# Attention in quarters of the TensorE array, interleaved score by value, in a fused attention and feed-forward kernel

## The chip, the cores and the metric

One core of a Trainium2 chip runs the whole program. The metric is the device time of one execution in microseconds; where several executions are given, it is their median.

## What is computed

```
q_n, k_n = rmsnorm(q, g_q), rmsnorm(k, g_k)       # 8 batches x 12 heads x 448 rows x 64, f32
scores   = q_n @ k_n.T / 8
attn     = exp(scores - max) / sum(exp(scores - max))
x        = (attn @ v), heads side by side          # 3584 x 768
h        = max(x @ w_in, 0)                        # 3584 x 2048
out      = (h * h) @ w_out                         # 3584 x 768
```

Everything is f32.

## The kernel before

**Units.** Attention is cut into 48 units `i` of two heads `e` (one batch, heads 2c and 2c+1). Scores are made transposed: keys on the partitions, the 448 queries along the row. The 448 keys of a head are three slots `m` of 128 keys and a rest of 64 keys; the rests of an even unit and of the odd one behind it share a fourth slot `NJ` (number 3). `score` (L426) multiplies kT by qT for both heads of a slot into two PSUM banks chosen by `banks_of` (L421), `weigh` (L439) has ScalarE (ACT) write exp of them to two `wT` tiles, `attend` (L506) multiplies v by these weights one unit later and adds over the slots in bank 4 (`values_bank`, L503). No maximum is subtracted in the branch that runs (`shift=False`); the gains are small enough. The sums of the weights are added up by GpSimd (POOL, `add_up`, L454), spread by matmuls with ones (`both_denominators`, L570, for two units at once), turned and moved out of PSUM by VectorE (DVE, `take_sums`, L604), inverted (`invert_both`, L579) and multiplied into x (`finish`, L647).

**Tiles of the array.** With 64 rows of d to contract, the two heads of a score use the upper and the lower 64 rows of the array at the same time, each with 128 columns (shape 64\*128). The values contract 128 keys and give 64 columns a head, so the two heads use the left and the right half (128\*64). The denominators use four strips of 32 columns (128\*32). Slot `NJ` uses quarters (64\*64), in `score` and in `attend_both` (L527). An f32 matmul stands in the trace as two records.

**The other work.** The feed-forward part uses products in the manner of Strassen: `first_products` or `deep_products` (L953; L982 is their matmul), then `second_products` (L1106; matmuls L1160, and L1098 in `multiply_rest`). These run in four blocks for each pair of batches, as a generator `ffn(u)`; DVE adds most products to SBUF (L1217, L967), ACT copies some (L979, L971). `deep_products` uses a bank aside, `banks[free_bank]`; `multiply_rest` uses banks 2 and 1. Banks 5 to 7 take the products in turn (`roles`).

**Order.** One program order is written out by hand. The main loop (L1690) runs the feed-forward generator up to a point (`run`, L1462, by planned costs and `place`, L1448), then makes one visit. Units up to 24 are visited in halves; from unit 25 on (`whole`, L275), one visit (`visit_whole`, L1640) does the scores of unit i and the values of unit i-1. Visits 25 to 47 are of this kind, visit 48 has the values of unit 47 alone. Three visits fall into each block; one of the three comes just behind `multiply_rest`. Visits 25 and 37 fall on the end of a pair of batches, where the generator is drained first.

Small work (turning q and k of the next unit, L365 on DVE and L367 on ACT; squares and their sums for a unit further on, L179 on ACT and L192 on DVE; inverting) stands in a deque `tasks`. One or two of these are issued with each step of the generator. `run_all` (L1487), at the start of each visit, issues all that are left. Between two points of each block the tasks are held back (`held`, L1057 to L1154), and the visit behind `multiply_rest` is the first to run them.

In `visit_whole` before, the order for TensorE is: scores of slots 0 and 1; values of slots 0, 1, 2 of the unit before; for odd i the values of slot `NJ` for units i-1 and i (`attend_both`), for even i the denominators of units i-2 and i-1; then the score of slot 2, and for even i of slot `NJ`. Scores use banks 0 to 3. For odd i, ACT then copies bank 0 and bank 4 to SBUF (L1661, L1663); the values of the odd unit are joined with that rest by DVE in `finish` (L652), as a task behind the next visit.

**Transfers.** All of them are issued by SyncE (SP), on one hardware queue. `transfers_of` (L310) puts a transfer in a list that is followed some at a time, one or two with each step of the generator. Loads of v (`load_v`, L370) go through that list; each is two transfers and one or two of `lasts`. `load_out` (L856) brings 1.5 MB of output weights and is issued directly, two calls for the next block, two steps after the end of a block (L1209, the list `later`).

## Time and profile before

| | us |
|---|---|
| median of 3 runs (1427.46 to 1429.78) | 1429.35 |
| profiled execution | 1425.93 |
| its span | 1424.1 |
| TensorE clock granted, share of full | 0.995 |
| TensorE matmul (PE) busy | 1389.0 |
| GpSimd (POOL) busy | 782.6 |
| VectorE (DVE) busy | 824.7 |
| ScalarE (ACT) busy | 583.2 |

The profile's page gives busy times, then the chain of work that ended last, then groups of instructions by line and shape. Ends of matmuls are modelled and overlap, so the starts of neighbouring matmuls are the better clock. A shape "64\*128 64x448" is a matmul with 64 rows and 128 columns of the array and 448 columns streamed.

### The profile page before, as it was taken

Reading aid. Unit: us, or ns where it says so; the run is one execution under the profiler, and the core shown is the slowest. Engines: PE = TensorE matmul, PEld = TensorE weight load, DVE = VectorE, ACT = ScalarE, POOL = GpSimd, SP = SyncE. Lnnn points to the kernel's source line nnn. Section 1 sums busy time; section 2 is a strip of 40 time slices with the busy share of each in tenths; the row PEclk is TensorE's granted clock in tenths of the full one; section 3 lists DMA queues with packets and bytes.
Section 4 is the critical chain, followed back from the end, with each engine's and each line's share of the span. In section 5 each row is a group of like instructions: output and inputs, shape, how many; then the busy total and the mean of one; then the engine's idle time right before and its main releaser. Section 6 shows DMA issues by size and latency. Waiting matters only on the chain.

```text
span 1424.1 us, 18297 instructions
## 1 busy us (share of the span) xinstructions
PE 1389.0 (98%) x5772; PEld 837.1 (59%) x5772; DVE 824.7 (58%) x1651; ACT 583.2 (41%) x1126; POOL 782.6 (55%) x778
## 2 busy tenths in 40 slices
PE   7999999999999999999999999999999999999998
PEld 3333444444444467584756757576675858778694
DVE  5997466877888854354444664344543565254444
ACT  6775466645646234452333423444333403221220
POOL 5666755654655877566574876655663654030311
PEclk9999999999999999999999999999999999999999
DMA  5555836857859875482736548374541716234132
GB/s 144 144 153 159 205 94 163 249 166 185 261 132 266 252 237 139 97 254 66 224 106 210 155 115 263 80 214 125 183 126 34 274 58 243 109 106 174 45 144 81
DMA packets 378927, 229.09 MB, mean 161 GB/s; under 512 B 271940, under 2 KB 347588, under 8 KB 374724
## 3 DMA queue, kind: packets, MB, share of 16 engines
q1 hardware_dynamic: 378528, 227.75, 55.1%
q8 instruction: 48, 0.79, 0.2%
q14 instruction: 59, 0.48, 0.1%
q10 hardware_dynamic: 292, 0.07, 0.0%
HBM read 172.49 MB, written 55.25 MB: 160 GB/s over the span
## 4 chain that ended last, share of the span: by engine, by line
PE 80%; DMA 4%; DVE 4%; POOL 3%; issue 3%; ACT 3%; SPq 3%; POOLq 0%; DVEq 0%; ACTq 0%
PE bank L1160 30%; PE bank L982 23%; PE bank L434 8%; PE bank L521 7%; PE bank L1098 5%; PE bank L928 4%; DMA vt<-in_v_dram 2%; DMA words<-in_moe_w_out_dram 1%; POOL sum L461 1%; SPq L316 1%; PE bank L533 1%; ACT wT L442 1%; PE bank L573 1%; PE bank L564 1%; DVE out_sb L1290 1%
## 5 line engine op out<-in xcount | busy, mean ns | idle before, releaser
L1217 DVE TENSOR_TENSOR acc<-acc,bank 128x384 f32<-128x384 f32 x324 | 173.9, 550 | 205.4 <-PE bank L1160 176.9
L982 PE MATMUL bank<-xT,in_sb 128*128 128x224 f32 x1344 | 288.0, 353 | 0.0
L1160 PE MATMUL bank<-out_sb,hid 128*128 128x384 f32 x768 | 270.9, 490 | 3.2 <-DVE acc L1217 2.5
L982 PEld LDWEIGHTS bank<-xT,in_sb 128*128 128x128 f32 x1344 | 252.7, 190 | 10.3 <-issue 3.9
L442 ACT ACTIVATE wT<-bank,rr 128x448 f32<-128x448 f32 x288 | 161.6, 631 | 124.6 <-PE bank L434 103.2
L1160 PE MATMUL bank<-out_sb,sums 128*128 128x384 f32 x576 | 207.4, 491 | 2.0 <-DVE acc L1217 1.9
L202 POOL TENSOR_TENSOR rr<-ms,minus_half 128x8 f32<-128x8 f32 (+1 forms) x96 | 147.8, 1540 | 111.7 <-DVE ms L195 90.1
L1160 PEld LDWEIGHTS bank<-out_sb,hid 128*128 128x128 f32 x768 | 145.0, 191 | 108.4 <-issue 6.5
L967 DVE TENSOR_TENSOR hid<-hid,bank 128x224 f32<-128x224 f32 x312 | 111.6, 383 | 128.8 <-PE bank L982 109.4
L434 PE MATMUL bank<-qT,kT 64*128 64x448 f32 (+1 forms) x768 | 172.5, 579 | 5.4 <-ACT part L442 3.4
L1160 PEld LDWEIGHTS bank<-out_sb,sums 128*128 128x128 f32 x576 | 107.5, 190 | 87.4 <-issue 6.9
L928 PE MATMUL bank<-xT,in_sb 128*128 128x448 f32 x336 | 131.9, 546 | 0.2 <-DVE hid L1068 0.2
L434 PEld LDWEIGHTS bank<-qT,kT 64*128 64x128 f32 (+1 forms) x768 | 59.3, 174 | 108.6 <-issue 70.2
L1035 POOL TENSOR_TENSOR hid<-hid 128x448 f32<-128x448 f32 x24 | 27.4, 1140 | 169.4 <-DVE hid L967 154.7
L461 POOL TENSOR_TENSOR sum<-sum,wT 128x448 f32<-128x448 f32 (+1 forms) x96 | 112.8, 1196 | 8.7 <-ACT wT L442 8.1
L521 PE MATMUL bank<-wT,vt 128*64 128x448 f32 x480 | 105.0, 550 | 3.7 <-DMA vt<-in_v_dram 3.7
L928 PEld LDWEIGHTS bank<-xT,in_sb 128*128 128x128 f32 x336 | 62.1, 190 | 69.2 <-issue 59.7
L461 POOL TENSOR_TENSOR sum<-wT 128x448 f32<-128x448 f32 x48 | 56.9, 1195 | 81.6 <-PE bank L573 80.7
L1039 ACT ACTIVATE hid<-hid 128x448 f32<-128x448 f32 x96 | 54.9, 572 | 83.5 <-DVE hid L967 54.2
L1098 PE MATMUL bank<-out_sb,hid 128*128 128x384 f32 x256 | 87.6, 488 | 0.0
L367 ACT ACTIVATE qT<-qT,g 128x448 f32<-128x448 f32 x34 | 22.7, 667 | 146.6 <-DVE qT L365 146.6
L982 PE MATMUL bank<-more,in_sb 128*128 128x224 f32 x288 | 74.4, 353 | 0.0
(130 smaller groups left out, 1854.4 us busy)
## 6 DMA issues: line engine op xcount, KB each, us to landing
out_sb<-out_forms SPq DMA_DIRECT2D x24, 1536.0 KB, 9.1
in_sb<-in_deep SPq DMA_DIRECT2D x64, 384.0 KB, 4.4
in_sb<-in_deep SPq DMA_DIRECT2D x80, 256.0 KB, 4.5
words<-in_moe_w_in_dram SPq DMA_DIRECT2D x32, 384.0 KB, 3.8
words<-in_moe_w_out_dram SPq DMA_DIRECT2D x32, 384.0 KB, 3.5
out_forms<-out_sb SPq DMA_DIRECT2D x8, 1536.0 KB, 6.6
qk<-in_q_dram SPq DMA_DIRECT2D x96, 96.0 KB, 2.8
qk<-in_k_dram SPq DMA_DIRECT2D x96, 96.0 KB, 2.8
```

What stands on the lines that cost most here:

```text
L202: self.nc.gpsimd.tensor_tensor(out=self.rr[i][:, x, 0 : self.count(i)], in0=ms, in1=self.minus_half.to_broadcast(list(ms.shape)), op=ALU.pow,)
L434: nc.tensor.matmul(sc[some], lhsT=turned[p, 1][r, keys], rhs=turned[p, 0][r, :], start=True, stop=True,)
L442: nc.scalar.activation(new_weights((i, m), e), sc, AF.Exp, scale=rows.rr[i][:, 1, 2 * m + e : 2 * m + e + 1],)
L461: nc.gpsimd.tensor_tensor(out=sums[i, e][some], in0=left[some], in1=weights[key_of(i, m), e][some], op=ALU.add)
L521: nc.tensor.matmul(values_bank(i)[ds(e * D, D), :], lhsT=lasts[i % 2][mine, e, :] if m == NJ else values[i][:, m, e, :], rhs=weights[key_o ...
L928: nc.tensor.matmul(ps, lhsT=w_sb[:, IN.index(left), c, :], rhs=forms[u, c][right], start=first and c == 0, stop=c == NK - 1, skip_group_ch ...
L967: nc.vector.tensor_tensor(out=quarter(name, n), in0=quarter(base, n), in1=ps, op=ALU.add)
L982: nc.tensor.matmul(ps, lhsT=left, rhs=right, start=start, stop=stop, skip_group_check=True)
L1039: nc.scalar.activation(dst, dst, AF.Relu)
L1098: nc.tensor.matmul(ps, lhsT=hid[a].rearrange("p t e s -> p t (e s)")[:, t, ds(NT * P, P)], rhs=w_sb[t][:, 2 * a + half, :], start=(a, t) = ...
L1160: nc.tensor.matmul(ps, lhsT=lefts[left][:, t, ts(tt, P)], rhs=w_sb[t][:, OUT.index(right), :], start=first and t == 0, stop=t == 1, skip_g ...
L1217: nc.vector.tensor_tensor(out=acc, in0=acc, in1=ps, op=ALU.add)
```

## The change

In visits from 25 on (and not in the other branch, `shift`):

- `score` makes slots 0 to 2 with four matmuls of 64\*64, by head and by half of the 128 keys.
- `attend_halves` makes the values of slots 0 to 2 with four matmuls of 64\*64, by half of the keys and by head; the lower 64 keys add up in bank 4, the upper 64 in bank 3. `join_halves` adds both banks (and the rest) in the visit itself.
- Values and scores alternate slot by slot. The denominators of an even visit come first, and in bank 2. Scores use banks (0, 1), (2, 0), (1, 2) and, for `NJ`, (0, 4).
- `free_bank` stays 1.
- `load_v` issues its transfers directly once the first pair of batches is through; `load_out` comes four steps behind a block, not two.

```
 def load_v(i):
-        queue = transfers_of("v", i)
+        queue = transfers_of("v", i) if first else nc.sync
...
 def banks_of(i, m):
-        first = 2 * m - 3 if whole(i) and m > 1 else m % 2 * 2
-        return [banks[(first + e) % 4][:, 0:S] for e in range(2)]
+        if whole(i) and not shift:
+            return [banks[n][:, 0:S] for n in ((0, 1), (2, 0), (1, 2), (0, 4))[m]]
+        return [banks[m % 2 * 2 + e][:, 0:S] for e in range(2)]
...
 def score(i, m):
+        if whole(i) and m < NJ:
+            for e, sc in enumerate(scs):
+                for half in range(2):
+                    nc.tensor.matmul(
+                        sc[ds(half * D, D)],
+                        lhsT=turned[i, 1][ds(e * D, D), ds(m * P + half * D, D)],
+                        rhs=turned[i, 0][ds(e * D, D), :], start=True, stop=True,
+                    )
+            return
...
+    def attend_halves(i, n):
+        for half, bank in enumerate((values_bank(i), second_bank(i))):
+            keys = ds(half * D, D)
+            for e in range(2):
+                nc.tensor.matmul(
+                    bank[ds(e * D, D), :], lhsT=values[i][keys, n, e, :],
+                    rhs=weights[(i, n), e][keys], start=n == 0, stop=n == NJ - 1 and (half or i % 2) == 1,
+                )
+    def join_halves(i):
+        xT = xts[pairs[i]] = new_x()
+        if i % 2:
+            nc.vector.tensor_tensor(out=xT, in0=values_bank(i), in1=rests.pop(i), op=ALU.add)
+        else:
+            nc.scalar.copy(rests[i + 1], banks[0][:, 0:S])
+            nc.scalar.copy(xT, values_bank(i))
+        nc.vector.tensor_tensor(out=xT, in0=xT, in1=second_bank(i), op=ALU.add)
...
-        later.append([2, lambda: [load_out(n + 2) for n in ns]])
+        later.append([4, lambda: [load_out(n + 2) for n in ns]])
...
 def visit_whole(i):
         run_all()
+            if i % 2 == 0:
+                both_denominators(i - 2)
+            for n in range(NJ):
+                attend(i - 1, (n,))
+                forget(i - 1, (n,))
+                if i <= last:
+                    score(i, n)
+                    weigh(i, n)
+            if i % 2:
+                attend(i - 1, (NJ,))
+                forget(i - 1, (NJ,))
+            join_halves(i - 1)
+            if i % 2 == 0:
+                tasks.append(lambda: invert_both(i - 2))
+                if i <= last:
+                    score(i, NJ)
+                    weigh(i, NJ)
```

`attend` calls `attend_halves` for slots 0 to 2 of these units, `second_bank` is bank 3, and `finish` no longer adds.

## The prediction, made before the changed kernel was run

> **What bounds the kernel.** I read the page first (busy times, then the chain that ended last), then the chain in order of time through the visits, then the timelines of PE, ACT and DVE around single visits.

> ```profile
> span 1424.1 us, 18297 instructions
> ...
> PE 1389.0 (98%) x5772; PEld 837.1 (59%) x5772; DVE 824.7 (58%) x1651; ACT 583.2 (41%) x1126; POOL 782.6 (55%) x778
> ...
> PE 80%; DMA 4%; DVE 4%; POOL 3%; issue 3%; ACT 3%; SPq 3%; POOLq 0%; DVEq 0%; ACTq 0%
> ```

> PE is the bound, with almost no idle time. So a gain has to come out of PE's own time: how densely matmuls follow one another, and the few waits. The chain in order of time (start, us, what, records) gives three visits, 43, 44 and the beginning of 45, and a transfer before visit 38:

> ```profile
> 855.14 11.55 DMA vt<-in_v_dram
> ...
> 1007.25 1.70 PE bank L434 x8
> 1008.95 2.40 PE bank L521 x12
> 1011.36 0.91 PE bank L533 x8
> 1012.27 0.95 PE bank L434 x4
> ...
> 1030.28 1.71 PE bank L434 x8
> 1031.99 2.41 PE bank L521 x12
> 1034.39 0.89 PE bank L573 x8
> 1035.28 1.90 PE bank L434 x12
> ...
> 1065.52 2.41 PE bank L434 x8
> ```

> A pass of 448 columns takes 0.375 us: weight loads of L521 start 0.37 to 0.38 apart in PE's timeline. Two matmuls side by side need two passes, 0.75. L521 (three such pairs) is 6 x 0.375 = 2.25, but 2.40 pass: 0.16 lie at its end, where the shape changes. L434 pays 0.20, L533 0.16, L573 0.14, and the 1.90 at the end of visit 44 (two pairs, two changes) 0.40. A change of shape costs 0.14 to 0.21; slots of one shape follow without a gap.

> Visit lengths, from the first matmul to the first of the products behind it (PE's timeline): quiet odd visits (29, 31, 35, 37, 41, 43, 47) 5.98, quiet even ones (28, 32, 34, 40, 44, 46) 6.90; directly behind `multiply_rest` (L1098) 7.6 (30, 36, 42) and 7.39, 6.96, 7.39, 6.92 (27, 33, 39, 45), as there slot 0's second head waits 0.7 for DVE to empty bank 1, hence the 2.41 above; 25, 26 and 38: 7.11, 8.17, 11.23.

> **The work itself: nothing.** A quarter matmul occupies a quarter of the array for the same 448 columns; four at once take 0.75, as a pair does. The quarter shape is in the trace: L533 does four in 0.91, which is 0.75 and one change, and

> ```profile
> 1095.29 0.24 PEld L434 LDWEIGHTS bank<-qT,kT 64*64 64x64 f32 x8 [0.65 <-issue]
> ```

> eight weight loads of quarters span 0.24 us in all, of 0.13 each. The visits get 564 more records (23 x 3 scores x 4 and 24 x 3 values x 4). [...] What the trace doesn't show is a quarter score directly behind a quarter value: between 0 (same shape: slots of one shape follow without a gap) and 0.17 each (L533's change). I take 0, the nearer row.

> **Changes of shape.** An even visit goes from five inside plus the exit to one (0.14, denominators to quarters) plus exit; an odd one from four (three inside, one to the products) to the exit alone. Entry: products before 64\*128 leave 0.05 more than before 64\*64 or narrower (0.33 against 0.24 to 0.28 behind L1160), for some 16 visits 0.8 us gained.

> **What is late next: exp.** Before, four score banks and 2.4 us of values stood between slot 0 and the first reuse of a bank. Now slot 1's second head needs bank 0, which slot 0's first exp must have read, and PE issues in order. From quiet even visits: exp starts 0.31 behind the end of its scores, takes 0.63, the next follows at 0.52; PE goes on 0.05 after. From that wait on, the lower half of the rows has four quarter groups left (slot 1 score, slot 2 value, slot 2 score, slot NJ): 4 x 0.75 = 3.0, and 0.2 to leave. So an odd visit lasts t + 0.67 + 3.2, t being when the first exp can start.

> - Quiet odd: scores of slot 0 end at 0.80 (first group after a change) + 0.75; t = 1.86; length 5.73 for 5.98. Six visits, **-1.5**. In 37 ACT is busy until 2.45 (L179): 6.3, **+0.3**.
> - Odd behind the rest (27, 33, 39, 45), and 25: here ACT is late, and was before, at no cost. Visit 45 started at 1065.45:

> ```profile
> 1066.61 0.52 ACT L179 ACTIVATE squares<-qk 128x384 f32<-128x384 f32 x1 [7.58 <-DVE ms L192]
> 1069.13 0.67 ACT L367 ACTIVATE qT<-qT,g 128x448 f32<-128x448 f32 x1 [2.00 <-DVE qT L365]
> 1069.71 2.19 ACT L442 ACTIVATE wT<-bank,rr 128x448 f32<-128x448 f32 x4
> ```

> `run_all` issues the held tasks first. The exps queue on ACT behind L367, which waits for DVE's turn, which stands behind L192, which waits for ACT's squares. t = 4.26 there (4.73, 4.29, 4.73 and 4.44 in 27, 33, 39, 25). None of that is edited. Lengths 8.1 to 8.6, together 41.8 for 35.8: **+6.0**. The eviction wait of 0.7 goes, as values come first, but inside this.
> - Even: denominators and slot 0's value come first, so t = 2.80, later than ACT's other work (at most 2.75, visit 36). The length is 0.80 + 0.14 + 0.80 + 6 x 0.75 + 0.2 = 6.44, 0.23 of waiting for bank 0, and 0.1 for DVE to free bank 4 ahead of slot NJ (its add takes 0.61, L652): 6.76. Six quiet ones **-0.8**; 30, 36, 42 lose the eviction wait, **-2.5**.
> - Denominators move up 4 us, ahead of everything. They need POOL's sums, which end 11 us or more before in the usual even visit and 2.3 us before in 38, so they don't wait. Visit 48: **+0.1**.

> **Transfers of v.** Before visit 38:

> ```profile
> 866.74 2.47 PE L521 MATMUL bank<-wT,vt 128*64 128x448 f32 x10 [3.38 <-DMA vt<-in_v_dram]
> ```

> SP's timeline has one half of v issued at 851.11, then two stores of outputs, both 1.5 MB loads of output weights at 853.36, and the other half of v at 855.14, landing 11.55 later behind them. Visit 26 waits likewise. Now v is issued whole first (its median landing is 3.2 us) and the large loads two steps later. The waits go; 26 and 38 become even visits of 6.76: -1.4 and -4.5, **-5.9**. The output weights have time: in the block that starts at 517 their first use is at 551.6, landing takes 9.1. Nothing else stands behind v on SP for more than two or three issues of 0.4 to 0.5.

> **After visits 25 and 37**, PE waits for ACT's copy of the first product, behind two exps and two copies:

> ```profile
> 849.03 0.65 PE L982 MATMUL bank<-words,in_sb 128*128 128x224 f32 x2 [0.44 <-ACT hid L979]
> ```

> By the starts of the matmuls 0.6 us are lost there and 0.5 behind 25. Now the exps and copies end 1.1 us behind the end of the visit (before: 2.1 in 37), and PE needs the first product's copy only 1.9 behind it: **-1.1**.

> **Other edits.** The joins add 24 DVE adds of 0.61 us and move twelve (L652). DVE is busy 58%, and behind an even visit's add it has nothing to do before the products. Behind an odd visit the add must wait for ACT's copy of x and ends 1.75 us behind the visit; the first eviction there starts at 1.6 (L1217, L1187), so it comes up to 0.2 late, which three banks in turn hide; without that cover 12 x 0.2 = 2.4 us. `free_bank` at 1: by the times above exp has read bank 1 at least 0.2 us before the products come. The x tile of an odd unit is taken some 10 to 20 us earlier; its cost I put at 0, with no row for it.

> **Sum.** -0.8 - 1.5 + 0.3 + 6.0 - 0.8 - 2.5 + 0.1 - 5.9 - 1.1 = -6.2. On the profiled execution 1425.93 - 6.2 = 1419.7. That execution is 3.4 below the median of the runs, 1429.35; on the median 1423.1. I forecast **1423**, 0.4% faster; terms off by half their size (6.0 and 5.9 are the largest) make it 1417 to 1429. Most of what the change of shapes could save is eaten by exp.

> **Rivals.**
> 1. *Quarter groups drain* where value and score alternate: six such places a visit, 138 in all, at L533's 0.17: +22.9, so 1446. For it: every change of line with a change of shape costs that much. Against: here the shape stays, and L434's slots follow each other without a gap. It turns the forecast into slower from 0.066 us a place ((6.2 + 2.9) / 138). Chance 0.12.
> 2. *The v loads still come late*, because something else on SP or on the queue stands ahead of them (a hidden transfer stays what it was): -6.2 + 5.9, so 1429. For it: the queue moves 1.5 MB pieces near those places anyway. Against: both waits have the two large loads directly ahead. Chance 0.13.
> 3. *Exp is late in more visits.* It is now on the path everywhere; half a us in each of 23 visits (bounds: 0 and the 2.4 to 2.9 of the late ones) is +11.5, so 1435. For it: quiet odd visits have 0.05 to 0.2 us between L179's end and t. Chance 0.12.
> 4. *Exp is not late behind the rest*, as tasks get done earlier: the five visits last 5.8 instead of 8.4, and the gain is near 19; if half of that comes, 1417. Chance 0.13.

> **Numbers.** Forecast 0.50. A measurement of this kernel can tell about 0.2%, 2.9 us, from no change. Faster: 0.47 of the forecast's chance and rival 4, 0.60. Same: rival 2 and what of the forecast and of rival 3 falls there, 0.18. Slower: rival 1 and most of rival 3, 0.22. The range goes from 1412 (rival 4 with the larger part of its gain) to 1435 (rival 3); rival 1 and little else lies outside.

> **What would show it.** Weight loads of quarters every 0.37 us through a visit, and no gap between `attend_halves` and `score` except where exp is awaited: right on shapes; gaps of 0.15 at each: rival 1. PE idle before slot 1's score, released by ACT, for about 1.9 us in 27, 33, 39, 45 and 25, and these visits at 8.1 to 8.6: right on exp. Quiet visits at 5.7 and 6.8. No wait for v in 26 and 38. Wrong would be idle time before the denominators (POOL's sums), DVE late for banks 3 and 4, or waits for output weights.

## The result and the profile after

| | before | after |
|---|---|---|
| median of 22 runs each, us | 1428.84 | 1429.86 |
| lowest and highest | 1425.93, 1431.17 | 1422.52, 1433.98 |
| profiled execution | 1425.93 | 1431.84 |
| its granted clock | 0.995 | 0.989 |

The ratio is 1.0004 [0.9993, 1.0015]: no change. Forecast were 1423 and "faster": the time lies in the forecast range of 1412 to 1435, but the gain of 6.2 us did not come. New line numbers: score in quarters L433, its rest L444, values in halves L548, `attend_both` L569, denominators L609, exp L452, deep products' matmul L1018, second products L1196, loads of `in_sb` L885, of output weights L895, of v L375 and L382.

The page of the changed kernel (busy times; then the shares of the chain that ended last):

```profile
span 1430.0 us, 19473 instructions
...
PE 1381.3 (97%) x6336; PEld 851.7 (60%) x6336; DVE 836.7 (59%) x1675; ACT 587.0 (41%) x1126; POOL 781.6 (55%) x778
...
PE 82%; DVE 5%; POOL 3%; DMA 3%; ACT 2%; issue 2%; SPq 2%; DVEq 0%; POOLq 0%; ACTq 0%
```

PE has 564 records more, as counted, and is busy 7.7 us *less*: the visits are denser. The span is 5.9 longer, so PE idles more: 48.7 us for 35.1. The chain in order of time through visit 43 and the beginning of 44, the same visits as shown of before:

```profile
1013.31 0.91 PE bank L548 x8
1014.22 0.75 PE bank L433 x8
1014.97 0.75 PE bank L548 x8
1015.72 0.94 PE bank L433 x8
1016.66 0.75 PE bank L548 x8
1017.41 0.78 PE bank L433 x8
1018.19 0.75 PE bank L569 x8
1018.94 4.07 PE bank L1196 x12
...
1036.01 0.89 PE bank L609 x8
1036.89 0.91 PE bank L548 x8
```

Each group of four quarters takes 0.75, as much as two passes, and value and score follow each other without a gap. Only the entry pays (0.91), and 0.19 waits for exp in slot 1's score (0.94). The visit lasts 5.64 for 5.98.

**Where the time went.** By the starts of the matmuls outside attention, which are the same in both kernels, from visit 25 on, after minus before in the profiled pair:

| | us |
|---|---|
| quiet odd visits (six), -0.27 to -0.36 each | -2.0 |
| quiet even visits (six), -0.31 to -0.34 each | -1.9 |
| 30, 36, 42 | -3.2 |
| 37 | +0.2 |
| ACT's copy behind 25 and 37, and one more at 789 of before | -1.6 |
| 25, 27, 33, 39, 45: wait for exp | +5.8 |
| v waits in 26 and 38 | -6.3 |
| waits for pieces of `in_sb`, 2.6 and 6.2 | +8.8 |
| half clock behind exp waits: 25, 27, 39 | +5.1 |
| half clock behind `in_sb` waits | +3.9 |
| half clock ahead of visit 25 (two windows less, one more) | -1.7 |

The last row is chance, as the two kernels are the same up to there. The rows add to +7.1; measured are +5.9, and 1.2 are spread over steps below 0.3. On the medians of the runs the difference is only +1.0: the profiled execution of before lies 2.9 below its median, that of after 2.0 above.

Three views carry this. First, visit 45: the timelines of ACT and PE (the bracket has the idle time before the instruction, and what ended it).

```profile
1073.17 0.92 PE L433 MATMUL bank<-qT,kT 64*64 64x448 f32 x4
...
1074.55 0.67 ACT L367 ACTIVATE qT<-qT,g 128x448 f32<-128x448 f32 x1 [2.00 <-DVE qT L365]
1075.12 2.34 ACT L452 ACTIVATE wT<-bank,rr 128x448 f32<-128x448 f32 x4
...
1075.79 0.59 PE L433 MATMUL bank<-qT,kT 64*64 64x448 f32 x2 [1.70 <-ACT wT L452]
```

Exp stands behind L367 on ACT as before, and now half of slot 1's score waits for it. Second, what PE waits for (us in total, times, longest):

```profile
PE bank L433 <- ACT wT L452: 9.7, 5, 2.2
PE bank L1018 <- DMA in_sb<-in_deep: 8.5, 2, 6.0
```

L433 <- ACT are the five visits forecast. No wait for v is left; in its place stand two waits for `in_sb`, the input weights that come in pieces, and both are in the blocks of visits 26 and 38. Third, SP's own timeline before the longer one (start, us, what):

```profile
855.00 1.93 SPq L895 DMA_DIRECT2D out_sb<-out_forms  x2
857.02 3.34 SPq L885 DMA_DIRECT2D in_sb<-in_deep  x4
860.46 9.57 SPq L324 DMA_DIRECT2D qk<-in_k_dram  x4
870.93 3.90 SPq L324 DMA_DIRECT2D qk<-in_q_dram  x4
...
882.57 1.01 SPq L375 DMA_DIRECT2D vt<-in_v_dram  x2
883.62 1.35 SPq L382 DMA_DIRECT2D lasts<-in_v_dram  x2
885.07 2.44 SPq L885 DMA_DIRECT2D in_sb<-in_deep  x5
```

`run_all` at visit 38 follows the whole list at once: from 860.46 to 882.5 SP issues q and k alone. Behind 3 MB of output weights four loads of k take 9.57 us to issue. The next pieces of `in_sb` go out at 885.07; the matmul before the gap had started at 882.98, and the next starts at 889.34:

```profile
889.34 1.09 PE L1018 MATMUL bank<-xT,in_sb 128*128 128x224 f32 x2 [6.01 <-DMA in_sb<-in_deep]
```

In before the same pieces went out from 880.38 on, two of them between the halves of v, and PE came to them later, because it had waited for v. SP's timeline of before:

```profile
862.40 5.37 SPq L324 DMA_DIRECT2D qk<-in_k_dram  x4
...
879.86 0.48 SPq L324 DMA_DIRECT2D vt<-in_v_dram  x1
880.38 0.96 SPq L849 DMA_DIRECT2D in_sb<-in_deep  x2
881.39 0.43 SPq L324 DMA_DIRECT2D vt<-in_v_dram  x1
881.87 1.34 SPq L324 DMA_DIRECT2D lasts<-in_v_dram  x2
883.31 1.50 SPq L849 DMA_DIRECT2D in_sb<-in_deep  x3
```

The piece that PE stands for in after is the second of them. In before it landed at 884.71, 1.7 us before PE came to it (886.40). In after it lands at 889.20, 4.5 later, and PE comes 3.2 earlier (883.2): 4.5 + 3.2 - 1.7 = 6.0, the gap. It is issued 4.8 later: 2.7 because the block of q and k ends at 882.53 instead of 879.82, 2.1 because both halves of v and the `lasts` now stand ahead of it.

### The profile page after: what moved, and what is told of

It is laid out like the page before. It is cut to its first block, busy times and chain, and to the rows that moved or that the text cites. A ratio compares the mean times of both kernels' runs of the same rounds, so it can differ in the third digit from the quotient of the medians.

```text
span 1430.0 us, 19473 instructions
## 1 busy us (share of the span) xinstructions
PE 1381.3 (97%) x6336; PEld 851.7 (60%) x6336; DVE 836.7 (59%) x1675; ACT 587.0 (41%) x1126; POOL 781.6 (55%) x778
## 4 chain that ended last, share of the span: by engine, by line
PE 82%; DVE 5%; POOL 3%; DMA 3%; ACT 2%; issue 2%; SPq 2%; DVEq 0%; POOLq 0%; ACTq 0%
PE bank L1196 30%; PE bank L1018 24%; PE bank L1134 5%; PE bank L964 5%; PE bank L444 4%; PE bank L433 4%; PE bank L548 4%; PE bank L534 4%; PE bank L583 1%; POOL sum L471 1%; PE bank L609 1%; ACT wT L452 1%; DVE out_sb L1326 1%; PE bank L600 1%; PE bank L569 1%
## 5 line engine op out<-in xcount | busy, mean ns | idle before, releaser
L1018 PE MATMUL bank<-xT,in_sb 128*128 128x224 f32 x1344 | 290.4, 355 | 8.5 <-DMA in_sb<-in_deep 8.5
L1196 PE MATMUL bank<-out_sb,hid 128*128 128x384 f32 x768 | 271.7, 491 | 3.7 <-DVE acc L1253 3.0
L1018 PEld LDWEIGHTS bank<-xT,in_sb 128*128 128x128 f32 x1344 | 253.9, 191 | 20.3 <-POOL sums L1120 6.3
L1196 PEld LDWEIGHTS bank<-out_sb,hid 128*128 128x128 f32 x768 | 145.7, 191 | 109.1 <-issue 7.2
L1196 PE MATMUL bank<-out_sb,sums 128*128 128x384 f32 x576 | 206.5, 490 | 2.0 <-DVE acc L1253 1.9
L452 ACT ACTIVATE wT<-bank,rr 128x448 f32<-128x448 f32 x288 | 164.1, 631 | 103.7 <-PE bank L444 56.1
L1196 PEld LDWEIGHTS bank<-out_sb,sums 128*128 128x128 f32 x576 | 107.5, 190 | 87.2 <-issue 5.0
L444 PE MATMUL bank<-qT,kT 64*128 64x448 f32 (+1 forms) x492 | 104.3, 582 | 5.2 <-ACT part L452 3.2
L433 PE MATMUL bank<-qT,kT 64*64 64x448 f32 x552 | 85.7, 559 | 9.7 <-ACT wT L452 9.7
L367 ACT ACTIVATE qT<-qT,g 128x448 f32<-128x448 f32 x34 | 22.7, 667 | 147.7 <-DVE qT L365 147.7
L548 PE MATMUL bank<-wT,vt 64*64 64x448 f32 x576 | 79.5, 557 | 0.0
L444 PEld LDWEIGHTS bank<-qT,kT 64*128 64x128 f32 (+1 forms) x492 | 35.6, 169 | 66.1 <-issue 39.8
```

The source lines that it names most:

```text
L433: nc.tensor.matmul(sc[ds(half * D, D)], lhsT=turned[i, 1][ds(e * D, D), ds(m * P + half * D, D)], rhs=turned[i, 0][ds(e * D, D), :], start ...
L444: nc.tensor.matmul(sc[some], lhsT=turned[p, 1][r, keys], rhs=turned[p, 0][r, :], start=True, stop=True,)
L452: nc.scalar.activation(new_weights((i, m), e), sc, AF.Exp, scale=rows.rr[i][:, 1, 2 * m + e : 2 * m + e + 1],)
L548: nc.tensor.matmul(bank[ds(e * D, D), :], lhsT=values[i][keys, n, e, :], rhs=weights[(i, n), e][keys], start=n == 0, stop=n == NJ - 1 and ...
L1018: nc.tensor.matmul(ps, lhsT=left, rhs=right, start=start, stop=stop, skip_group_check=True)
L1196: nc.tensor.matmul(ps, lhsT=lefts[left][:, t, ts(tt, P)], rhs=w_sb[t][:, OUT.index(right), :], start=first and t == 0, stop=t == 1, skip_g ...
```

## The experiments

Each is timed against the kernel before on the same chip (4 to 12 runs of it, 9 to 34 of before). "Clock" is the mean granted TensorE clock of the runs; before has 0.995 to 0.996 in these sets. In the expectations, theory A says that the edits of transfers swap the waits for v for waits for `in_sb`; its numbered forms differ in what makes `in_sb` late. Its rival B puts the loss into the quarters. C puts the missing gain into ACT's order ahead of exp, and E says that idle time of PE halves the clock behind it. A "gap" is measured from the start of one matmul to the start of the next; a "wait" is the idle time that the view of waits gives, some 0.35 less.

**quarters_only.** Attention as changed, both edits of transfers undone:

```
-        queue = transfers_of("v", i) if first else nc.sync
+        queue = transfers_of("v", i)
...
-        later.append([4, lambda: [load_out(n + 2) for n in ns]])
+        later.append([2, lambda: [load_out(n + 2) for n in ns]])
```

> The changed kernel with both transfer edits undone: v goes through the list again, output weights two steps behind a block. Theory A (the wait for v was the DMA queue's own lateness; once TensorE doesn't spend it on v, it spends it, and more, on the in_sb pieces, 2.6 us before 552 and 6.2 us before 889, and the clock halves behind those waits): the waits for v in visits 26 and 38 come back (about 6 us in all), the waits for in_sb go below 1 us in all, and with the half clock behind them gone the kernel is 1 to 7 us faster than the changed one. Rival B (the transfer edits brought the 5.9 us forecast, and what is lost lies in the attention visits alone): 4 to 6 us slower than the changed kernel. Both: the odd visits 25, 27, 33, 39, 45 stay at 8 to 10 us, the quiet ones at 5.6 and 6.6.

1428.81 for 1427.36, 1.0009 [0.9999, 1.0018]; clock 0.991. What PE waits for:

```profile
PE bank L433 <- ACT wT L452: 9.6, 5, 2.2
PE bank L548 <- DMA vt<-in_v_dram: 6.1, 2, 4.1
```

The v waits are back (visits 26 and 38 last 11.0 and 14.0, half clock behind them included, for 8.2 and 11.2 in before) and the `in_sb` waits are gone. So the quarters with the old transfers bring no gain either: what the shapes save is spent on exp, on half clock and on a longer wait for v. B's 4 to 6 us more than the changed kernel did not come. Neither did the 1 to 7 us less that A expected: A had the two waits right, but not the half clock, which now stands behind the waits for v.

**transfers_only.** The kernel before, with the two lines above as in the change.

> The kernel before with the two transfer edits alone. Theory A: visits 26 and 38 lose their waits for v (5.9 us), and waits for in_sb of 5 us or more in all appear near 550 and 887; the time is within 3 us of before, or slower by up to 5 if the clock halves there. Rival B: no wait for in_sb, 1423, 5 to 6 us faster than before.

1429.62, 1.0015 [1.0003, 1.0026]; clock 0.994. Visits 26 and 38 last 6.90, as quiet ones, and PE waits for `in_sb` instead, in gaps of 2.92 and 5.11 with half clock behind both. The exchange doesn't need the quarters. (The view of waits puts the longer gap down to POOL, an add of which ended just then, 888.73. The piece of `in_sb` landed at 888.62, 0.13 before the matmul, as in after, where 0.14 lie between; and in `v_in_list` the same matmul started with fewer of POOL's adds done. The same holds for the 7.1 of `out_2_steps` below and for the second wait of `gain_dve_list`, 2.9.)

**out_2_steps.** The change, output weights two steps behind the block again (v direct).

> The changed kernel with only the output weights back at two steps behind a block; v still at once. Theory A1 (the queue as a whole is late, whatever comes first): the waits for in_sb stay at 7 to 10 us in all, the time within 2 us of the changed kernel. Theory A2 (the later output weights push the q and k loads and the pieces behind them back): the waits for in_sb fall below 5 us, and the kernel is 3 us or more faster than the changed one.

1429.08, 1.0021 [1.0009, 1.0033]; clock 0.990. Gaps for `in_sb` of 1.13 and 7.1: 8.2 in all, nearly as much as in the change (2.80 and 6.36, together 9.2). The place of the output weights alone doesn't make the wait.

**v_in_list.** The change, v through the list again (output weights at four steps).

> The changed kernel with only v back in the list; output weights still four steps behind a block. Theory A3 (v issued at once takes SP's time ahead of the in_sb pieces: two v and one or two lasts, 1.6 to 2.4 us): the pieces are issued about 2 us earlier, the waits for in_sb fall from 8.8 to 4 to 6 us in all, v waits stay below 1 us since the second half of v now goes ahead of the output weights, and the kernel is 3 to 5 us faster than the changed one. Theory A1 (the queue as a whole): within 2 us of the changed kernel.

1422.86, 0.9967 [0.9957, 0.9978]; clock 0.993. The `in_sb` waits shrink from 8.5 to 4.0, and no v wait comes back (26 and 38 last 6.56 and 6.58). Either edit of transfers alone takes the v wait away (`out_2_steps` has none either); v issued directly, ahead of the pieces, is the one that costs.

**gain_dve_list.** `v_in_list`, and in whole units DVE, not ACT, multiplies turned q by the gain (L367):

```
-            nc.scalar.mul(dst, dst, g)
+            if whole(i):
+                nc.vector.tensor_scalar(out=dst, in0=dst, scalar1=g, scalar2=None, op0=ALU.mult)
+            else:
+                nc.scalar.mul(dst, dst, g)
```

> v_in_list (v in the list, output weights four steps behind) and one edit more: for units from 25 on, DVE and not ACT multiplies the turned q by the gain, so that no exp stands behind that instruction on ACT. Theory C (exp is late in visits 25, 27, 33, 39, 45 because ACT waits in order for DVE's turned q, and the half clock comes behind TensorE's wait for exp): the first exp starts 1.8 to 2.2 us into those visits, they last 5.6 to 6.1 us instead of 8.1 to 10.3, the half clock behind them is gone, and the kernel is 10 to 14 us faster than v_in_list, near 1411. Part of the 4 us that visit 25 gains is taken back by the in_sb wait near 550. Rival D (the exps there wait for something else, a bank, a weight tile or the squares): these visits stay above 7.5 us and the time within 3 us of v_in_list.

1411.56, 0.9893 [0.9876, 0.9909]; clock 0.994. ACT's timeline in visit 45:

```profile
1053.07 0.52 ACT L179 ACTIVATE squares<-qk 128x384 f32<-128x384 f32 x1 [7.56 <-DVE ms L192]
1053.68 1.16 ACT L455 ACTIVATE wT<-bank,rr 128x448 f32<-128x448 f32 x2
1055.19 1.16 ACT L455 ACTIVATE wT<-bank,rr 128x448 f32<-128x448 f32 x2 [0.34 <-PE bank L436]
```

Exp follows the squares directly. Visits 25, 27, 33, 39, 45 last 5.6 to 5.9 for 8.1 to 10.3, without half clock. So one instruction of 0.67 us on ACT, with what it waited for, held back 11 us. (The multiplication stays, on another engine.)

**before_gain_on_dve.** The same edit in the kernel before.

> The kernel before with DVE and not ACT multiplying the turned q by the gain for units from 25 on. Theory C says that exp is late there too, but covered by four score banks and the values: the visits keep their lengths within 0.1 us, and the time stays within 2 us. Rival: late exps cost time before as well; more than 3 us faster.

1427.13, 0.9995 [0.9985, 1.0006]. No gain, as expected, but the visits don't keep their lengths: 25 gets 1.1 shorter, 27, 33, 39 and 45 0.2 to 0.8, together 3.2. In the profiled pair visits 26 and 38 take that back by waiting longer for v (11.7 and 14.1 for 8.2 and 11.2, half clock included). ACT's order cost that kernel little, and what it cost is hidden behind v.

**fill_exp_wait.** `v_in_list` with six matmuls of no use (their results are never read) where PE waits for exp:

```
+                    if n == 1 and i in (25, 27, 33, 39, 45):
+                        for _ in range(3):
+                            for e in range(2):
+                                nc.tensor.matmul(
+                                    roles[2][ds(e * D, D), 0:S], lhsT=values[i - 1][0:D, 2, e, :],
+                                    rhs=weights[(i - 1, 2), e][0:D], start=True, stop=True,
+                                )
```

> v_in_list with six extra matmuls of 64*64 (2.25 us on the upper half of the rows, their result never read) ahead of the score of slot 1 in visits 25, 27, 33, 39, 45, in the time in which TensorE waits for exp. Theory E (the half clock is the price of TensorE's idle time there): these visits last 8.1 to 8.6 us in every one of the five, no half clock between 500 and 520, 565 and 580, 900 and 915; 3 to 5 us faster than v_in_list in the mean. Rival F (the half clock comes from something else, as the load of the quarter shape): the half clock stays behind at least two of the visits, same time as v_in_list.

1419.36, 0.9944 [0.9931, 0.9958]; clock 0.996. More work, and a shorter time: visits 25 and 39 last 8.29 and 8.55 for 9.96 and 10.25, the wait filled but no shorter. The full clock around 25 and 39 (stretch, its length, then busy time and count of PE, PEld, DVE, ACT, POOL, then PEclk, the share of DMA and GB/s):

```profile
500.00:520.00 20.00, 20.00 (x122) 13.38 (x121) 11.77 (x24) 8.80 (x17) 14.79 (x15) 1.00 0.61 146
...
895.00:915.00 20.00, 20.00 (x88) 10.46 (x85) 7.07 (x16) 8.56 (x16) 13.68 (x12) 1.00 0.43 85
```

PEclk is 1.00 in both stretches; in after it is 0.50 behind both visits (511.5 to 514.9 and 910.9 to 914.3). So here half clock came with the idle time itself and was a cost on top of the wait.

**gain_dve_out12.** `gain_dve_list` with the output weights twelve steps behind the block.

> gain_dve_list with the output weights twelve steps behind a block instead of four. Theory A4 (the 3 MB of output weights ahead of the q and k loads and of the in_sb pieces on the one queue make the pieces late): the waits for in_sb near 550 and 885 fall below 1.5 us in all, the half clock there goes, and the kernel is 3 to 6 us faster than gain_dve_list. Rival A5 (SP's order of issue makes them late, the q and k block at the start of visits 26 and 38): the waits stay above 4 us in all, and the time within 2 us. Rival A6: the products behind 550 and 885 wait for the output weights instead.

1430.84, 1.0026 [1.0011, 1.0041]; clock 0.990. Neither A4 nor a rival holds: all six blocks now wait for `in_sb`, 19.9 us in all, and the time is 19 us longer than that of `gain_dve_list`.

```profile
PE bank L1021 <- DMA in_sb<-in_deep: 19.9, 6, 5.0
```

**out_3_steps.** The same with three steps.

> gain_dve_list with the output weights three steps behind a block instead of four. Twelve steps brought waits for in_sb in every block; if earlier is better throughout (the large loads then run while TensorE's pieces are still ahead), 1 to 3 us faster than gain_dve_list and no wait for v in 26 and 38, as v's second half goes one step ahead; if the step doesn't matter between two and four, the same within 1.5 us.

1410.13, 0.9876 [0.9856, 0.9897]. Not to be told from four steps. The pieces still come late twice (gaps 2.55 and 2.27): the step isn't the lever.

**no_flush.** `gain_dve_list`, and at visits 26 and 38 `run_all` issues the tasks but doesn't follow the whole list:

```
-    def run_all():
+    def run_all(flush=True):
...
-        if not first:
+        if not first and flush:
             follow_transfers(len(transfers))
...
-        run_all()
+        run_all(i not in (26, 38))
```

> gain_dve_list without following the whole list of transfers at the start of visits 26 and 38; the q and k transfers there go one with each step. Theory A5 (SP issues in order, and the block of q and k transfers at these two visits stands ahead of the in_sb pieces for about 19 us): the waits for in_sb near 547 and 875, 2.2 and 3.2 us in gain_dve_list, fall below 1 us each, the half clock behind them goes, and the kernel is 4 to 9 us faster than gain_dve_list, near 1405. Rival A1 (the queue as a whole has too much to move between a drain and the next pieces): the waits stay above 2 us each, the time within 2 us.

1403.26 for 1426.88, 0.9835 [0.9817, 0.9853]; clock 0.997: the best version. SP's timeline behind the first of the two visits:

```profile
523.67 7.68 SPq L324 DMA_DIRECT2D qk<-in_k_dram  x4
533.21 0.82 SPq L888 DMA_DIRECT2D in_sb<-in_deep  x2
534.12 2.95 SPq L324 DMA_DIRECT2D qk<-in_q_dram  x4
537.37 1.31 SPq L888 DMA_DIRECT2D in_sb<-in_deep  x3
```

Pieces now go out between the loads of q and k. No wait for `in_sb` is left, and no half clock between 120 us and the last 1.5.

**after_no_flush.** That edit alone on the changed kernel.

> The changed kernel with one edit: the list of transfers isn't followed as a whole at the start of visits 26 and 38. Theory A5 (the block of q and k transfers ahead of the in_sb pieces on SP is the cause of the in_sb waits, whatever v and the output weights do): both waits (2.6 and 6.2 us) fall below 1 us, the half clock behind them (552 to 556, 887 to 894) goes, visits 25, 27, 39 stay at 8.3 to 10.3, and the kernel is 9 to 14 us faster than the changed one, near 1418. Rival: v issued at once still delays the pieces; one of the waits stays above 2 us.

1416.41 for 1426.4, 0.9921 [0.9906, 0.9937]; clock 0.996. No wait for `in_sb`, the exp waits as they were. The flush cost the change some 12 us (0.9921 against 1.0004).

**before_no_flush.** That edit alone on the kernel before.

> The kernel before with the same one edit. Theory A5: the pieces were in time there, as TensorE waited for v first; the waits for v, behind the output weights, stay near 1.3 and 4.3 us; within 2 us of before. Rival: the block of transfers also made v late; the waits for v go, 4 to 6 us faster.

1426.84, 1.0000 [0.9989, 1.0010]. The v waits stay: visits 26 and 38 last 8.8 and, with half clock, 14.1. Before, the flush was under the cover of v.

## Why the prediction was wrong, and where it was right

- **The work itself, changes of shape: right.** Groups of four quarters take 0.75 and leave no gap (chain of visit 43). In PE's weight loads, value and score alternate 0.37 to 0.38 apart:

```profile
1119.56 0.21 PEld L548 LDWEIGHTS bank<-wT,vt 64*64 64x64 f32 x8 [0.28 <-issue]
1119.98 0.15 PEld L433 LDWEIGHTS bank<-qT,kT 64*64 64x64 f32 x4 [0.22 <-issue]
```

  Rival 1 (0.17 at each of 138 places, which makes 23.5 rather than 22.9) is out. Nor did the number of records show as a cost: PE's busy time fell by 7.7 us with 564 records more, and eight records of quarters take 0.75 us, 94 ns each.
- **Quiet visits: right in sign, too small.** Odd and even ones were forecast -2.3 and brought -3.9. The -0.8 for the entry brought nothing: from the start of the last product to that of the visit's first matmul it is 0.42 or 0.28 us in both kernels. 30, 36 and 42 brought -3.2 for -2.5; 37 +0.2 for +0.3. Rival 3 (exp late in more visits) is out.
- **Exp late behind the rest: right in size, +5.8 for +6.0.** Visits 33 and 45 last 8.08 (forecast 8.16 and 8.13), and, free of half clock, 27 lasts 8.55 in `v_in_list` (8.60) and 25 8.29 in `fill_exp_wait` (8.31). Rival 4 is out, but `gain_dve_list` shows that its number was there to be had.
- **ACT's copies: right**, -1.1 for the two named; a third, -0.6, was missed.
- **"The waits go": the v waits did (-6.3 for -5.9), the time did not.** The failed step is the sentence "Nothing else stands behind v on SP for more than two or three issues", with the cost of nothing that was drawn from it. As a count it is about right (2.1 us in SP's order). It leaves out how much time the transfers behind v have: the pieces of `in_sb`, needed some 14 us behind either visit, had 1.7 us to spare behind visit 38, and only because PE had waited for v; and the flush stood ahead of them too. Without the wait PE comes 3.2 us earlier, and SP issues the pieces 4.8 later. +8.8 came back as waits. The time is that of rival 2 (1429) by luck, as the mechanism is another: v is in time, and what is behind it is late. `transfers_only` shows the exchange alone, `after_no_flush` takes it away.
- **The clock: no term at all.** The sum counted every idle us once. Behind waits of 1.91 (visit 25) and 2.17 us (27, 39) the granted clock went from 1.00 to 0.50 for 3.41 us in after, so that each cost 1.7 more: +5.1 behind the exp waits, and +3.9 behind those for `in_sb`. In the mean of its runs after has a clock of 0.991, and before has 0.995 to 0.996; 0.004 to 0.005 of 1425 is 6 to 7 us, about the forecast gain (6.2). `fill_exp_wait`, which removes idle time but no wait, gains 3.3 us on `v_in_list` (0.9944 against 0.9967). That is the price of two half-clock windows, 1.7 each, and in the profiles two are gone, those behind visits 25 and 39: the causal test. (The waits for `in_sb` also fell there, from 4.0 to 2.9.)

On the profiled pair the forecast was -6.2 and the result +5.9, 12.1 apart: +8.8 for `in_sb` and +7.3 for the clock, which had no term; -2.8 as the terms that had one came out better than forecast, and -1.2 that are not traced.

Not tried was v issued directly with no flush and the gain on DVE together. Why four loads of k take 9.57 us to issue behind the output weights is known in part. In none of the 14 profiles, where the landing is known, does an issue of SP start before the transfer eight places ahead of it has landed: in before and after that is 908 issues each, the closest 0.016 us behind the landing, while 77 and 71 of 909 start before the transfer seven places ahead has landed. In before two loads of k start at 862.40 and 866.40, just behind the landing of the two large loads (862.34 and 866.38); in `no_flush` at 526.30 and 530.03 (526.29 and 530.02); in after at 864.40 and 869.71 (864.36 and 869.70). In after, though, the second and third issue themselves take 3.24 and 4.67, and why is open; so is what ties an issue to the landing eight places ahead.

## What to carry to other kernels

Here a wait on the critical engine (3.38 us for v in visit 38) was cover for what stood behind it: before counting the removal of one as a gain, list the transfers due in the next block and the time at which each is issued, and see who is next. The list that was emptied in one go ahead of a visit (860.46 to 882.5 in after) stood ahead of what other code issued directly on the queue; spreading it was worth 12 us in the changed kernel, 8 in `gain_dve_list`, and nothing in the kernel whose earlier wait hid it. Look also at the issue eight places behind a large load: in after two loads of k started 0.04 and 0.01 us behind the landing of such loads. With scores and values interleaved as here, exp came onto the critical path (five waits, 9.7 us): what stood ahead of it on its engine had to leave first, which gained 11 us, and idle time of TensorE is to be priced with the clock that followed it, 1.7 us for each window at half clock.

## What the runs showed of the hardware that was not expected

```profile
508.10:511.50 3.40, 1.49 (x18) 0.62 (x20) 0.92 (x2) 2.43 (x5) 3.32 (x5) 1.00 0.25 69
511.50:514.90 3.40, 3.40 (x20) 0.93 (x12) 0.00 (x0) 1.71 (x3) 3.32 (x4) 0.50 0.44 73
736.80:740.20 3.40, 2.32 (x26) 1.04 (x28) 0.00 (x0) 3.20 (x6) 2.33 (x3) 1.00 0.78 169
740.20:743.60 3.40, 3.40 (x16) 1.75 (x11) 1.08 (x2) 2.27 (x5) 3.27 (x3) 1.00 0.25 56
907.50:910.90 3.40, 1.23 (x12) 0.35 (x10) 1.80 (x4) 1.52 (x3) 3.04 (x3) 1.00 0.51 88
910.90:914.30 3.40, 3.40 (x24) 1.19 (x18) 0.00 (x0) 1.87 (x4) 2.44 (x3) 0.50 0.61 153
```

Behind 1.91 and 2.17 us of idle time in a window the clock of the next is halved (1.00 turns to 0.50), behind 1.08 it isn't. Over the 14 profiles, between 480 and 1200 us, 34 windows at full clock had 1.83 us or more of idle time, and 33 of them were followed by half clock (the other had 1.90); 20 had 0.9 to 1.81, and one of them was (1.66). Of these the profiles of before and after have 5 of the 34, all followed by half clock, and 4 of the 20, none followed by it. A wait that the border of two windows split, with less than 1.83 on either side, was free of it here: in the kernel before, the wait of 3.38 us for v fell so in the profiled execution, 1.57 and 1.81 to a side of the border at 864.93 (the windows below are cut at 864.9):

```profile
861.50:864.90 3.40, 1.86 (x8) 0.38 (x4) 0.54 (x1) 2.24 (x4) 2.42 (x2) 1.00 1.00 401
864.90:868.30 3.40, 1.56 (x9) 0.63 (x10) 0.00 (x0) 0.56 (x1) 0.00 (x0) 1.00 1.03 354
868.30:871.70 3.40, 3.40 (x24) 0.83 (x21) 0.65 (x1) 0.69 (x3) 1.13 (x1) 1.00 0.86 160
```

In the profile of `before_no_flush` the wait in the same place, 3.6 us, fell otherwise, 2.2 and 1.5 to a side, and 6.8 us of half clock followed. With this agree the wait for exp at 33 and 45 (1.70, of which at most 1.07 lie in one window), which cost nothing more, and visit 27, which lasted 10.25 in after and 8.55 in `v_in_list` with a wait of the same length (2.17): in after it lies in one window, in `v_in_list` 0.76 and 1.41 lie to a side of a border. That the runs of the changed kernel spread with the clock (1422.52 at 0.995, 1433.98 at 0.988) fits it, but only one of them has a trace.
